# Attention kernel: two PSUM tiles of one bank in place of one tile of two banks, and a normalising step in two halves, one step later

## The chip, the cores and the metric

One core of one Trainium2 chip runs the whole program. The metric is the time of one execution on the device in microseconds (us). The engines have their own in-order queues and run side by side: TensorE (PE) multiplies and transposes, VectorE (DVE) and ScalarE (ACT) do elementwise work, GpSimd (POOL) does small elementwise work, SyncE (SP) issues DMA transfers. PE writes its results to PSUM, which is divided into banks of 512 float32 values per partition; DVE and ACT read them from there.

## The reference

Three blocks follow each other; only the first is touched by the change. It is attention over 4 batches and 8 heads, with 576 positions and heads of 64 values, and a threshold in place of a full softmax:

```python
scores = scale * np.matmul(q, k.transpose(0, 1, 3, 2))
thresh = np.max(scores, axis=-1, keepdims=True) - tau
scores = np.where(scores >= thresh, scores, -1000000000.0)
scores = scores - np.max(scores, axis=-1, keepdims=True)
attn = np.exp(scores)
attn = attn / (np.sum(attn, axis=-1, keepdims=True) + 1e-09)
return np.matmul(attn, v)
```

Its output, as a table of 2304 tokens by 512 values, goes through a gated block (two products, a sigmoid, a product) and a second block with another activation, both with weights in float32.

## The kernel before

Attention works on **pairs of heads** (p = 0 to 15) and, in each pair, on five **units** u: units 0 to 3 are 128 query rows of both heads, unit 4 is the 64 rows left over of each head, stacked. One turn of the loop at L384 is a **step**; a step starts unit u of pair p and carries older units on. The order of the instructions on each engine is the order in which the code issues them; a scheduling layer adds only the waits between engines. In one step, in this order:

- PE multiplies queries with keys for the new unit (`scores`, L245, for unit 4 L241) into two PSUM tiles, transposes the masked exponents of the unit from two steps ago (`turns`: L288 for the first 512 keys, into the wide tile; L289 for the last 64 keys of both heads, into `left`), and multiplies transposed exponents with values (`attend`, L312), into `av`. Once a pair, in the step of unit 2, L401 also transposes the row sums into another part of `left`.
- DVE scales the scores and takes their extreme (`maxima`, L254), then, for the unit of the step before, makes the masked exponents and their sum (`masks`, L274).
- ACT copies the transposes out of PSUM (`copies`: L294 and L298, for unit 4 twice L303 and L304; L298 and L304 read `left`), then takes the exponentials of the new unit (`exponents`, L266), then, when a round of products with values is complete, copies it out of `av` (`drain`, L322), and once a pair copies the row sums out of `left` (`sum_rows`, L331).
- POOL makes the thresholds (L257), copies the last keys' exponents together (`lt`, L281), and once a pair multiplies a finished pair of heads by the reciprocals of its sums (`normalise`, L342), which came back by DMA (`spread`, L339).

The products with values of a pair come in two rounds (table at L378): round 0 is complete in the step in which the next pair starts unit 1, round 1 in the step in which it starts unit 4. Both rounds use the same place `av`, so the first product of a round has to wait until the drain of the round before is done. `left` and `av` are the two halves of one tile `aw`, each half one bank. Parts of the later blocks' work (weights split into two words, L138 and L148 to L162) are spread over the attention steps, one piece in the step of unit 0 of each pair.

Step 0, step 1 and so on below mean the step in which a pair starts unit 0, unit 1 and so on.

Of the kernel before, what the change touches and what calls it, by code (L numbers as in the profile page):

```python
# [10 lines left out]
F32 = mybir.dt.float32  # L11
# [3 lines left out]
ALU = mybir.AluOpType  # L15
AX = mybir.AxisListType
PSUM = bass.MemoryType.PSUM
# [12 lines left out]
def kernel(  # L30
# [17 lines left out]
    nc = tc.nc  # L48
# [3 lines left out]
    NP, _, S = q.shape  # L52
# [5 lines left out]
    P = 128  # L58
    HS = S // 2
# [8 lines left out]
    pool = lambda n, b, **kw: tc.tile_pool(name=n, bufs=b, **kw)  # L68
# [14 lines left out]
    rbs = [const.tile([P, S], F32, name=f"rb_{i}") for i in range(2)]  # L83
# [109 lines left out]
    def attention():  # L193
# [2 lines left out]


        ps_o = ctx.enter_context(ExitStack())
        aw = ps_o.enter_context(pool("ps_o", 1, space=PSUM)).tile([P, 2, 512], F32, name="aw")
        left, av = aw[:, 0], aw[:, 1]  # L200
        wa, wb, wt = wides
        st1, st2 = (ctx.enter_context(ExitStack()) for _ in range(2))
        sb1 = lambda n, b: st1.enter_context(pool(n, b))
# [5 lines left out]
        N = NP * U  # L209
# [7 lines left out]
        def load(p):  # L217
            t = qkp.tile([P, 2, S], F32, tag="qk", name="qk")
            nc.sync.dma_start(out=t[:, 0], in_=q[p])
            nc.sync.dma_start(out=t[:, 1], in_=k[p])  # L220
            qk[p] = t

        def load_v(p):

            t = vs[p % 3]
            for e in range(2):
                es = slice(e * R, e * R + R)
                nc.sync.dma_start(out=t[:, e, :nf], in_=v[p][:, e * (nf + 1) : e * (nf + 1) + nf])
                nc.sync.dma_start(out=t[es, e, nf], in_=v[p][es, nf])

        def corner(p):
            for e in range(2):
                es = slice(e * R, e * R + R)
                nc.gpsimd.tensor_copy(corners[p % 2][es, es], qk[p][es, 0, nf * P :])

        def scores(p, u):
            t = qk[p]
            for s in range(2):
                c = slice(s * HS, s * HS + HS)
                if u == nf:  # L240
                    nc.tensor.matmul(wa[:, s, :HS], corners[p % 2], t[:, 1, c], start=True, stop=True)  # L241
                    continue
                for e, w in enumerate((wa, wb)):
                    es = slice(e * D, e * D + D)
                    nc.tensor.matmul(  # L245
                        w[:, s, :HS], t[es, 0, u * P : u * P + P], t[es, 1, c], start=True, stop=True
                    )

        def maxima(p, u):

            t = sp.tile([P, 2, 2, HS], F32, tag="s", name="s")
            mx = mxs[(p * U + u) % 2]
            for e, w in enumerate((wa, wb)[: 1 if u == nf else 2]):
                nc.vector.tensor_scalar(  # L254
                    t[:, e], w[:, :, :HS], nscale, None, op0=ALU.mult, op1=ALU.min, accum_out=mx[:, 0, e : e + 1]
                )
                nc.gpsimd.tensor_scalar(  # L257
                    mx[:, 1, e : e + 1], mx[:, 0, e : e + 1], tau_b, None, op0=ALU.add
                )
            st[p, u] = t, mx  # L260

        def exponents(p, u):
            t, mx = st[p, u]
            ex = pe_.tile([P, 2, 2, HS], F32, tag="ex", name="ex")
            for e in range(1 if u == nf else 2):
                nc.scalar.activation(ex[:, e], t[:, e], AF.Exp, scale=-1.0, bias=mx[:, 0, e : e + 1])  # L266
            st[p, u] = t, mx, ex
# [15 lines left out]
        def turns(p, u):  # L283
            pr = pt.pop((p, u))
            for e in range(1 if u == nf else 2):
                for c in range(nf):
                    cs = slice(c * P, c * P + P)
                    nc.tensor.transpose(wt[:, e, cs], pr[:, e, cs], ident)  # L288
            nc.tensor.transpose(left[:, :P], lts.pop((p, u)).rearrange("p a b -> p (a b)"), ident)  # L289

        def copies(p, u):
            r, o = min(u // 2, 1), u % 2 * P if u < nf else 2 * P
            if u < nf:
                nc.scalar.activation(  # L294
                    rt[r].rearrange("p e c n -> p (e c) n")[:, :, o : o + P],
                    wt.rearrange("p e (c n) -> p (e c) n", n=P), AF.Copy,
                )
                nc.scalar.activation(rl[r][:, o : o + P], left[:, :P], AF.Copy)  # L298
                return
            for e in range(2):  # L300
                es = slice(e * R, e * R + R)
                x = wt[:, 0].rearrange("p (c n) -> p c n", n=P)
                nc.scalar.activation(rt[r][:, e, :, o : o + R], x[:, :, es], AF.Copy)  # L303
                nc.scalar.activation(rl[r][es, o : o + R], left[es, es], AF.Copy)  # L304

        def attend(p, r, cs):


            n = NR[r]
            for c in cs:  # L310
                for e in range(2):
                    nc.tensor.matmul(  # L312
                        av[e * D : e * D + D, :n], vs[p % 3][:, e, c], rt[r][:, e, c] if c < nf else rl[r],
                        start=c == 0, stop=c == nf,
                    )

        def x_of(p):
            b, hp = divmod(p, NHP)
            return xall[:, hp, b * S : (b + 1) * S]

        def drain(p, r):
            nc.scalar.activation(x_of(p)[:, r * NR[0] : r * NR[0] + NR[r]], av[:, : NR[r]], AF.Copy)  # L322

        def denom(p):
            rs = sums[p % 2]
            nc.vector.reciprocal(rs, rs)

        def sum_rows(p):

            n = 2 * nf + 1  # L330
            nc.scalar.activation(rows[p % 2][:n], left[:n, P : 2 * P], AF.Copy)  # L331
            drs[p] = dram.tile([n, P], F32, tag="dr", name="dr")
            nc.sync.dma_start(out=drs[p], in_=rows[p % 2][:n])
# [4 lines left out]
                src = bass.AP(tensor=dr.tensor, offset=dr.offset + o, ap=[[a, 2], [0, D], [1, n]])  # L338
                nc.sync.dma_start(out=rbs[p % 2][:, (o > 0) * nf * P :][:, :n], in_=src)  # L339

        def normalise(p):
            nc.gpsimd.tensor_tensor(x_of(p), x_of(p), rbs[p % 2], op=ALU.mult)  # L342

        def background():

# [35 lines left out]
        for p in range(NP):  # L381
            for i, (r, a, b) in (rounds if p + 1 < NP else final).items():
                parts.setdefault(p * U + i, []).append((p, r, range(a, b)))
        for t in range(N + 7):  # L384
            p, u = divmod(t, U)
            on = t < N
            mk = divmod(t - 1, U) if 1 <= t <= N else None
            at = divmod(t - 2, U) if 2 <= t <= N + 1 else None

            pd, ud = divmod(t - U, U)  # L390
            pd2, ud2 = divmod(t - 2 * U, U)
            if ud2 == 1 and 0 <= pd2 < NP:
                normalise(pd2)
            if on:
                scores(p, u)
            if t == N + 1:
                yield t - N, True
            if at:
                turns(*at)
            if ud == 2 and 0 <= pd < NP:  # L400
                nc.tensor.transpose(left[: 2 * nf + 1, P : 2 * P], sums[pd % 2], ident)  # L401
            for part in parts.get(t, ()):
                attend(*part)
            if on:
                maxima(p, u)
            if at:
                copies(*at)
            if on:
                exponents(p, u)
            if ud == 1 and 0 <= pd < NP:  # L410
                denom(pd)
            if on and u == 0 and p > 0:
                if p < 13:
                    next(bg, None)
                else:
                    yield t - N, "gap"
            if ud == 2 and 0 <= pd < NP:
                sum_rows(pd)
            for part in parts.get(t, ()):
                if part[2][-1] == nf:  # L420
                    drain(*part[:2])
            if mk:
                masks(*mk)
                if mk[1] == nf:
                    nc.gpsimd.tensor_scalar(sums[mk[0] % 2], sums[mk[0] % 2], 1e-9, None, op0=ALU.add)
            if on:
                if u == 1 and p + 1 < NP:
                    corner(p + 1)
                if u == 2 and p + 2 < NP:
                    load(p + 2)  # L430
                if u == 4 and p + 2 < NP:
                    load_v(p + 2)
                if t == 1 or u == 2 and p % 2 == 0 and p < 12:
                    next(bg, None)
            if ud == 3 and 0 <= pd < NP:
                spread(pd)
            if t == N - 1:
                wides[:] = [wb, wa, wt]
            if t == N:
                run(bg)  # L440
                nc.scalar.activation(dummy, half, AF.Sigmoid)
                st1.close()
            if t == N + 2:
                st2.close()
                ps_o.close()
            yield t - N, False
# [267 lines left out]
```

## Time and profile before

| | us |
|---|---|
| median of 3 runs (1171.86 to 1172.95) | 1172.07 |
| time of the profiled execution | 1175.26 |
| span of the profiled execution | 1173.1 |
| PE busy in the span | 1137.0 (97%) |
| DVE busy | 804.2 (69%) |
| ACT busy | 563.5 (48%) |
| POOL busy | 139.9 (12%) |

The median is from runs without the profiler; the profiled execution is another one. Attention takes up the first 310 us or so of the span; a pair of heads takes about 18.4 us there. The rest belongs to the two later blocks. Busy shares over the whole span mix these stages, so what follows reads the attention stage by itself.

### The profile page before, as it was taken

What the parts mean: (1) busy time and instruction counts of PE and PEld (TensorE: products, weight loads), DVE (VectorE), ACT (ScalarE), POOL (GpSimd) and SP (SyncE); (2) the same over time, 40 slices, a digit from 0 to 9 for tenths busy, and PEclk for the clock granted to TensorE, in tenths of its full rate; (3) what the DMA queues carried; (4) which work ended last, traced back from release to release, by engine and by line L of the source; (5) the groups of instructions that cost most, each with busy time, mean ns of one, the idle gap of its engine ahead of it and who ended that gap; (6) DMA issues with size and microseconds to landing.
All of it is one profiled execution on the core that took longest, in us unless ns stands there. A gap on an engine that the chain in (4) does not pass through costs nothing.

```text
span 1173.1 us, 17522 instructions
## 1 busy us (share of the span) xinstructions
PE 1137.0 (97%) x6516; PEld 969.1 (83%) x6516; DVE 804.2 (69%) x1491; ACT 563.5 (48%) x1027; POOL 139.9 (12%) x299
## 2 busy tenths in 40 slices
PE   8999999998899999999999999999999999999998
PEld 5555555555689999999999999998989898989897
DVE  6888888888499998756667654455556555575554
ACT  5777777777534434333344332344345434353433
POOL 3444444445100000000000000000000000000000
PEclk8999999999989999999999999999999999999999
DMA  3232232220556556444344324112110512041201
GB/s 127 81 79 71 70 100 63 61 73 21 176 182 211 179 180 225 157 166 162 135 162 161 138 87 142 39 54 67 60 54 16 177 60 64 27 152 65 62 11 54
DMA packets 59380, 122.31 MB, mean 104 GB/s; under 512 B 8976, under 2 KB 35232, under 8 KB 59296
## 3 DMA queue, kind: packets, MB, share of 16 engines
q1 hardware_dynamic: 59152, 121.20, 31.6%
q8 instruction: 51, 0.84, 0.3%
q14 instruction: 33, 0.27, 0.1%
q10 hardware_dynamic: 144, 0.00, 0.0%
HBM read 98.57 MB, written 22.62 MB: 103 GB/s over the span
## 4 chain that ended last, share of the span: by engine, by line
PE 85%; DVE 9%; ACT 2%; issue 2%; DMA 1%; POOL 0%; DVEq 0%; SPq 0%; POOLq 0%; ACTq 0%
PE w L562 17%; PE w L554 13%; PE pgv L471 8%; PE pgv L473 8%; PE pgv L472 8%; PE pu L473 6%; PE pu L472 6%; PE pu L471 6%; PE aw L312 5%; PE w L245 4%; DVE s L254 3%; PE w L288 3%; DVE p L274 2%; PE w L241 1%; ACT ex L266 1%
## 5 line engine op out<-in xcount | busy, mean ns | idle before, releaser
L471 PE MATMUL pgv<-xflat,ih 128*128 128x384 f32 x560 | 188.6, 337 | 6.1 <-ACT act L513 4.2
L473 PE MATMUL pgv<-xflat,il 128*128 128x384 f32 x560 | 188.3, 336 | 0.0
L472 PE MATMUL pgv<-xflat,ih 128*128 128x384 f32 x560 | 188.3, 336 | 0.0
L528 ACT ACTIVATE hh<-act 128x384 fp32r<-128x384 f32 x168 | 88.5, 527 | 180.8 <-DVE act L517 119.0
L254 DVE TENSOR_SCALAR_CACHE_REDUCE s<-w,nscale 128x576 f32<-128x576 f32 x144 | 112.7, 816 | 40.4 <-PE w L245 28.9
L524 ACT ACTIVATE act<-act,half 128x384 f32<-128x384 f32 x96 | 59.2, 617 | 167.7 <-DVE act L521 167.7
L530 DVE TENSOR_TENSOR hl<-act,hh 128x384 fp32r<-128x384 f32 x168 | 93.5, 557 | 62.0 <-ACT hh L528 62.0
L473 PE MATMUL pu<-xflat,il 128*128 128x384 f32 x384 | 128.9, 336 | 0.0
L472 PE MATMUL pu<-xflat,ih 128*128 128x384 f32 x384 | 128.9, 336 | 0.0
L471 PE MATMUL pu<-xflat,ih 128*128 128x384 f32 x384 | 128.5, 335 | 0.0
L517 DVE TENSOR_TENSOR act<-pgv,act 128x384 f32<-128x384 f32 x70 | 38.9, 555 | 118.8 <-PE pgv L473 115.2
L274 DVE SCALAR_TENSOR_TENSOR p<-s,mx,ex 128x576 f32<-128x576 f32 x144 | 119.0, 859 | 0.5 <-POOL lt L281 0.5
L562 PE MATMUL w<-oh,hh 128*128 128x512 f32 x288 | 113.9, 395 | 0.4 <-DVE xall L585 0.4
L562 PE MATMUL w<-ol,hh 128*128 128x512 f32 x288 | 114.0, 396 | 0.0
L562 PE MATMUL w<-oh,hl 128*128 128x512 f32 x288 | 113.9, 396 | 0.0
L471 PEld LDWEIGHTS pgv<-xflat,ih 128*128 128x128 f32 x560 | 105.9, 189 | 8.5 <-ACT act L513 4.8
L266 ACT ACTIVATE ex<-s,mx 128x576 f32<-128x576 f32 x144 | 104.5, 770 | 6.7 <-DVE s L254 6.3
L472 PEld LDWEIGHTS pgv<-xflat,ih 128*128 128x128 f32 x560 | 106.0, 189 | 1.8 <-DVE xflat L463 0.2
L473 PEld LDWEIGHTS pgv<-xflat,il 128*128 128x128 f32 x560 | 105.8, 189 | 0.0
L525 DVE TENSOR_TENSOR act<-pu,act 128x384 f32<-128x384 f32 x96 | 53.5, 558 | 70.2 <-ACT act L524 70.2
L288 PEld LDWEIGHTS w<-ident,p 128*128 128x128 f32 x576 | 63.5, 142 | 43.2 <-ACT ex L266 31.2
L513 ACT ACTIVATE act<-pgv 128x384 f32<-128x384 f32 x70 | 34.2, 489 | 134.7 <-PE pgv L473 134.5
(82 smaller groups left out, 2189.3 us busy)
## 6 DMA issues: line engine op xcount, KB each, us to landing
w<-saved SPq DMA_DIRECT2D x48, 512.0 KB
w<-saved SPq DMA_DIRECT2D x24, 768.0 KB
raw<-in_moe_w_out_dram SPq DMA_DIRECT2D x28, 512.0 KB
saved<-w SPq DMA_DIRECT2D x12, 768.0 KB
raw<-in_moe_w_in_dram SPq DMA_DIRECT2D x16, 512.0 KB
saved<-w SPq DMA_DIRECT2D x16, 512.0 KB
raw<-in_moe_w_gate_dram SPq DMA_DIRECT2D x12, 512.0 KB
raw<-in_moe_w_val_dram SPq DMA_DIRECT2D x12, 512.0 KB
```

What stands on the lines that cost most here:

```text
L254: nc.vector.tensor_scalar(t[:, e], w[:, :, :HS], nscale, None, op0=ALU.mult, op1=ALU.min, accum_out=mx[:, 0, e : e + 1])
L266: nc.scalar.activation(ex[:, e], t[:, e], AF.Exp, scale=-1.0, bias=mx[:, 0, e : e + 1])
L274: nc.vector.scalar_tensor_tensor(pr[:, e], t[:, e].rearrange("p a b -> p (a b)"), mx[:, 1, e : e + 1], ex[:, e].rearrange("p a b -> p (a b ...
L288: nc.tensor.transpose(wt[:, e, cs], pr[:, e, cs], ident)
L471: nc.tensor.matmul(ps, ih[:, i, kk], xh[:, kk, c], start=(kk == 0), stop=False)
L472: nc.tensor.matmul(ps, ih[:, i, kk], xl[:, kk, c], start=False, stop=False)
L473: nc.tensor.matmul(ps, il[:, i, kk], xh[:, kk, c], start=False, stop=(kk == KD - 1))
L524: nc.scalar.activation(act, act, AF.Square, scale=0.5, bias=half)
L528: nc.scalar.activation(hh[:, c], act, AF.Copy)
L530: nc.vector.tensor_tensor(hl_[:, c], act, f32(hh[:, c]), op=ALU.subtract)
L554: nc.tensor.matmul(at(y, a, b), l[:, ds_], r[:, c], start=new and m == 0, stop=last and m == 2, skip_group_check=True,)
L562: nc.tensor.matmul(y[i % 3][:, i // 3], l[:, ts_], r, start=first and m == 0, stop=last and m == 2,)
```

## The change

The tile `aw` of two banks becomes two tiles `left` and `av` of one bank each, in the same pool. The multiplication by the reciprocals, one instruction over 576 columns in step 1 two pairs later, becomes two instructions over 288 columns, one in step 2 and one in step 3. The loop runs two turns longer so that the last pair gets both halves. From L341 on the line numbers of the kernel after are higher by one.

```diff
-        aw = ps_o.enter_context(pool("ps_o", 1, space=PSUM)).tile([P, 2, 512], F32, name="aw")
-        left, av = aw[:, 0], aw[:, 1]
+        banks = ps_o.enter_context(pool("ps_o", 1, space=PSUM))
+        left, av = (banks.tile([P, 512], F32, name=n) for n in ("left", "av"))
...
-        def normalise(p):
-            nc.gpsimd.tensor_tensor(x_of(p), x_of(p), rbs[p % 2], op=ALU.mult)
+        def normalise(p, s):
+            x, c = x_of(p), slice(s * HS, s * HS + HS)
+            nc.gpsimd.tensor_tensor(x[:, c], x[:, c], rbs[p % 2][:, c], op=ALU.mult)
...
-        for t in range(N + 7):
+        for t in range(N + 9):
...
-            if ud2 == 1 and 0 <= pd2 < NP:
-                normalise(pd2)
+            if ud2 in (2, 3) and 0 <= pd2 < NP:
+                normalise(pd2, ud2 - 2)
```

On POOL, this is the stretch from step 1 to step 3 of one pair before (`xall` is the attention output, `rb` the reciprocals, `mx` the thresholds, `corner` the stacked queries of unit 4):

```order
L342 TENSOR_TENSOR xall<-xall,rb_80 128x576
L257 TENSOR_SCALAR mx_83<-mx_83,tau_b 128x1 x2
L281 COPY lt<-p 128x128
L234 COPY corner_81<-qk 64x64 x2
L257 TENSOR_SCALAR mx_84<-mx_84,tau_b 128x1 x2
L281 COPY lt<-p 128x128
L257 TENSOR_SCALAR mx_83<-mx_83,tau_b 128x1 x2
```

The same stretch of the kernel after:

```order
L257 TENSOR_SCALAR mx_83<-mx_83,tau_b 128x1 x2
L281 COPY lt<-p 128x128
L234 COPY corner_81<-qk 64x64 x2
L343 TENSOR_TENSOR xall<-xall,rb_80 128x288
L257 TENSOR_SCALAR mx_84<-mx_84,tau_b 128x1 x2
L281 COPY lt<-p 128x128
L343 TENSOR_TENSOR xall<-xall,rb_80 128x288
L257 TENSOR_SCALAR mx_83<-mx_83,tau_b 128x1 x2
```

The multiplication no longer stands ahead of the thresholds of step 1; a half of it stands behind the corner copies, and the other behind the `lt` copy of step 2.

On PE, this is the middle of step 2 before, with the semaphores that each instruction waits for in brackets (`w_123` is the wide tile, `p` the masked exponents, `r` their transposes, `v` the values):

```order
L288 MATMUL w_123<-ident,p 128x128 [waits DVE_49]
L288 MATMUL w_123<-ident,p 128x128 x3
L289 MATMUL aw<-ident,lt 128x128 [waits Activation_49,Pool_49]
L401 MATMUL aw<-ident,sum_87 9x128
L312 MATMUL aw<-r_159,v_164 64x320 x4
```

The same place in the kernel after:

```order
L288 MATMUL w_123<-ident,p 128x128 [waits DVE_49]
L288 MATMUL w_123<-ident,p 128x128 x3
L289 MATMUL left<-ident,lt 128x128 [waits Activation_49,Pool_49]
L402 MATMUL left<-ident,sum_87 9x128
L312 MATMUL av<-r_160,v_165 64x320 [waits Activation_49]
L312 MATMUL av<-r_160,v_165 64x320 x3
```

The first product with values now has a wait for ACT of its own, which before stood two instructions ahead of it, on the transpose into the other bank. The order of PE's instructions is the same.

## Rows read from the trace of the kernel before

**Rows 1.** Window: us, busy PE, PEld, DVE, ACT, POOL, PE clock, DMA share, GB/s.
```profile
200.00:250.00 50.00, 46.34 (x328) 28.53 (x326) 43.78 (x108) 36.72 (x69) 23.61 (x47) 1.00 0.27 72
```

**Rows 2.** Waits of PE, 30 to 310 us: total us, times, longest.
```profile
PE w L288 <- DVE p L274: 9.2, 11, 1.0
PE aw L289 <- POOL mx L257: 5.0, 8, 0.6
PE aw L289 <- ACT xall L322: 3.7, 8, 0.6
```

**Rows 3.** Waits of ACT, 30 to 310 us.
```profile
ACT rl L298 <- PE aw L312: 20.6, 31, 1.8
ACT rl L304 <- PE aw L312: 16.9, 14, 1.2
```

**Rows 4.** Timeline, steps 1 and 2 of one pair: start, us, engine, line, count, [idle before].
```profile
211.13 0.27 PE L289 MATMUL aw<-ident,lt 128*128 128x128 f32 x1
211.33 1.08 PE L312 MATMUL aw<-r,v 128*64 128x256 f32 x8
211.33 0.38 ACT L303 ACTIVATE r<-w 128x256 f32<-128x256 f32 x1 [0.87 <-PE w L288]
...
212.92 0.22 ACT L304 ACTIVATE rl<-aw 64x64 f32<-64x64 f32 x1 [1.21 <-PE aw L312]
...
213.68 1.44 ACT L266 ACTIVATE ex<-s,mx 128x576 f32<-128x576 f32 x2
...
213.95 1.24 PE L288 MATMUL w<-ident,p 128*128 128x128 f32 x8
...
214.61 0.29 POOL L281 COPY lt<-p 128x128 f32<-128x128 f32 x1
...
215.15 0.38 ACT L322 ACTIVATE xall<-aw 128x256 f32<-128x256 f32 x1
...
215.67 0.30 PE L289 MATMUL aw<-ident,lt 128*128 128x128 f32 x1 [0.49 <-ACT xall L322]
...
216.01 1.30 PE L312 MATMUL aw<-r,v 128*64 128x320 f32 x8
```

**Rows 5.** Timeline, step 3 of the same pair.
```profile
218.41 1.09 PE L288 MATMUL w<-ident,p 128*128 128x128 f32 x8
218.51 0.82 DVE L254 TENSOR_SCALAR_CACHE_REDUCE s<-w,nscale 128x576 f32<-128x576 f32 x1 [0.86 <-PE w L245]
...
219.34 0.27 PE L289 MATMUL aw<-ident,lt 128*128 128x128 f32 x1
```

**Rows 6.** Timeline, step 2 of the first such pair.
```profile
30.73 1.10 PE L288 MATMUL w<-ident,p 128*128 128x128 f32 x8
32.45 0.30 PE L289 MATMUL aw<-ident,lt 128*128 128x128 f32 x1 [0.62 <-ACT xall L322]
```

**Rows 7.** Timeline, step 2 of the last such pair.
```profile
287.68 1.09 PE L288 MATMUL w<-ident,p 128*128 128x128 f32 x8
...
288.87 0.38 ACT L322 ACTIVATE xall<-aw 128x256 f32<-128x256 f32 x1
...
289.40 0.30 PE L289 MATMUL aw<-ident,lt 128*128 128x128 f32 x1 [0.62 <-POOL mx L257]
```

**Rows 8.** Timeline, DVE and POOL in step 1 of the pair of rows 4.
```profile
211.39 0.81 DVE L254 TENSOR_SCALAR_CACHE_REDUCE s<-w,nscale 128x576 f32<-128x576 f32 x1
211.71 1.41 POOL L342 TENSOR_TENSOR xall<-xall,rb 128x576 f32<-128x576 f32 x1 [0.42 <-DMA rb<-dr]
212.25 1.48 DVE L274 SCALAR_TENSOR_TENSOR p<-s,mx,ex 128x576 f32<-128x576 f32 x1
```

**Rows 9.** All masks of the kernel: shortest, median, longest, in ns.
```profile
L274 DVE SCALAR_TENSOR_TENSOR p<-s,mx,ex x144: 759/815/1625, 11.1 to 298.6; 128x576 f32<-128x576 f32 x144
```

**Rows 10.** Timeline of ACT at the end of attention.
```profile
311.62 0.27 ACT L331 ACTIVATE row<-aw 9x128 f32<-9x128 f32 x1 [3.54 <-PE aw L312]
311.80 0.41 ACT L322 ACTIVATE xall<-aw 128x320 f32<-128x320 f32 x1
```

## The prediction

> **What bounds the kernel now.** I read the attention stage alone, since the diff touches nothing else: first the busy times by window, then PE's waits, then ACT's, then the timeline of one pair. The window shows PE busy for 46.34 of 50 us at a granted clock of 1.00 (its level of 2.4 GHz), DVE for 43.78 [rows 1]. Two engines are nearly full, so what matters is where PE stands still all the same. Its waits fall into two places [rows 2]: L288 in step 1, where DVE's masks come late (9.2 us in 11 times), and L289 in step 2 (5.0 and 3.7 us, 16 times, one per pair). The change touches the second.
>
> Follow the second back in one pair [rows 4]. L289 starts at 215.67, right after the drain L322 ended (215.15 + 0.38 = 215.53). The drain stands on ACT behind the two exponentials L266 (213.68), these behind the copies L303 and L304, and the first L304 stood idle for 1.21 us until L312 was through, at about 212.9. But L304 reads `left`, which L289 had finished at 211.13 + 0.27 = 211.40; L312 writes the other bank. So both ends of this chain are waits that the data doesn't ask for: L304 for products in `av`, and L289 for the drain of `av`. ACT's waits show that it is so everywhere: L298 and L304 wait for L312 45 times [rows 3]. In 8 pairs the wait view names POOL's L257 as what ended L289's wait; the drain does there too, for in the last pair it ends at 288.87 + 0.38 = 289.25 and L289 starts 0.15 us later [rows 7], against 0.14 in rows 4.
>
> **The split of the tile.** It removes both waits. I work the pair of rows 4 through.
>
> ACT: L303 starts at 211.33 and ends at 211.71; L304 can follow at once. From the first L304 to the first L266 it took 213.68 - 212.92 = 0.76 us, so L266 starts at 212.47 in place of 213.68. Its scores are there: the second L254 of that step ends at 211.39 + 0.81 = 212.20 [rows 8]. The drain follows 215.15 - 213.68 = 1.47 later, at 213.94, and ends at 214.32, 1.21 us earlier. The products that it reads end at 212.9, so its new wait for PE is met.
>
> PE: step 2 reaches L288 at 213.95. How long from there to L289 if nothing waits? Step 3 shows it: 219.34 - 218.41 = 0.93 us, against 215.67 - 213.95 = 1.72 in step 2 [rows 4, 5]. So L289 starts at 214.88, and the pair gains 0.79 us. The new wait, of L312 for the drain, costs nothing: L312 comes 216.01 - 215.67 = 0.34 after L289, at 215.22, and the drain ended at 214.32. What is queued behind L312 on PE are the next step's scores, which DVE waits for; they move 0.79 forward. What is late next? The copy `lt`, which ended at 214.61 + 0.29 = 214.90 [rows 4]: level with the new start of L289. It follows a mask which the other part of the change lets go up to 0.66 us earlier (below), so it won't hold.
>
> Does the gain stay? From step 3 to step 0 of the next pair PE has no wait in the wait view, so what it gains in step 2 it carries forward. DVE must keep up: it stands idle 0.86 us before the first L254 of step 3, waiting for PE [rows 5]. PE comes 0.79 earlier and the masks ahead of it about 0.56 (0.66, less a short wait for scores), so 0.63 us of idling stays. The other wait, L288 in step 1, stays as it is: it hangs on DVE's work after the scores of step 0, and these move along with PE.
>
> The distance from L288 to L289 in step 2 is 1.72 us in 13 of the 15 pairs that have it (32.45 - 30.73 in the first, 289.40 - 287.68 in the last [rows 6, 7]), and 0.03 and 0.08 less in the other two. The sum is 15 x 0.79 - 0.11 = 11.7 us. The sixteenth entry of rows 2 is in the last steps; there the wait is 0.15 us and I count nothing.
>
> At the end of attention L331 waits for L312 although its row sums are long there, and the drain L322 stands behind it [rows 10]. L331 will be done before; the drain starts at 311.62 and no longer at 311.80, and with it ACT's first work for the next block, queued behind: 0.2 us.
>
> What it adds: a wait on the first L312 of each round. Those of step 0 already have a wait for a DMA and so get a wait instruction. L289 waits for two engines in every step, and step 3's 0.93 us holds that wait, already met, so I take 0. The ends are 0 and what a wait takes to let PE go when it is met late, 0.14 us in rows 4: 15 x 0.14 = 2.1 us.
>
> **The normalising.** Before, L342 runs on POOL from 211.71 to 213.12, and the mask L274 beside it takes 1.48 us in place of the median of 0.815: 0.66 more, while the L254 that also runs beside it keeps its 0.81 [rows 8, 9]. So a POOL multiplication holds up a mask, and not a maximum. Without it DVE is 0.66 earlier with that pair of masks, and then waits for the scores of step 2. In step 3 the waiting L254 starts 0.10 us after PE's L288 [rows 5], so here it starts at 213.95 + 0.10 = 214.05. That is what lets `lt` go earlier (above). The delay was hidden by the drain; with the drain gone it would have kept about 0.1 us in this pair. The move thus protects the 0.79 more than it adds.
>
> Where do the halves fall? Half of 1.41 is 0.71 us. The first stands behind the corner copies; POOL gets there about 0.9 us after the last mask of step 1, which is at about 214.7, while DVE runs its two L254 of step 2 (214.05 to 215.5). The second stands behind the `lt` copy of step 2, at about 217.5, when DVE idles or runs the L254 of step 3. So neither is beside a mask, and both cost 0. The ends are 0 and 0.71 us for each half that does hold up a mask. The thresholds behind them are wanted a step later, and the reciprocals, for which L342 still stood idle 0.42 us, have one step more.
>
> The trace agrees with the lock that the Trainium skill describes (SBUF — State Buffer, "Who interferes with whom"): a DVE instruction with two inputs from SBUF and a GpSimd instruction that reads SBUF exclude each other, and the one that starts first holds the port to its end. By that rule cutting one instruction in two makes two occasions for a mask to be held; if both take one, that is the third rival below.
>
> **Sum.** 11.7 + 0.2 = 11.9 us less. The profiled execution took 1175.26 us, 3.2 more than the median of the plain runs; from it 1163.4, and against the median of 1172.07 it is **1160.2 us**.
>
> **Rivals.**
> 1. The wait only moves. If the exponentials of step 1 start late for another reason, the drain ends when it did, and L312 waits in place of L289. Then L289 and L401 run under the wait, 0.34 us a pair: 15 x 0.34 = 5.1, 1167.0 us. For it: the drain still stands behind two exponentials. Against: I find 214.32 against a need at 215.22, so 0.9 us would have to go wrong.
> 2. DVE becomes the bound. It is 88% busy, and of its idle time in step 3 I leave 0.63 us. If half of the gain is lost that way, it is 15 x 0.4 = 6 us, 1166 us. Against: all of DVE's waits in steps 3, 4 and 0 are for PE.
> 3. The port: each half starts just before a mask and holds it up for 0.71 us. That is 1.41 a pair, less DVE's 0.63 of idling, 0.78, which cancels the 0.79: 1172 us. For it: a half and the masks of step 1 are 0.1 us apart on my timetable. Against: even if the first half does hit, its delay lies within the 0.63.
> 4. Slower: PE is held while ACT reads `left`. Before, no L298 or L304 ran beside L312, so no row shows this pair. If every such read stops PE for its length (four of 0.28 us and two of 0.22 in a pair), that is 1.56 a pair, 15 x (1.56 - 0.79) = 11.6 us more, 1183.7 us; it decides from half of that price on. Against: L303 reads PSUM beside L312 in rows 4 with no gap in PE, and L294 reads it beside L312 in every other step.
> 5. The waits are not what they look like, and the split changes nothing: 1172 us. Against: the new program has the waits at their new places.
>
> **How the numbers follow.** The forecast 0.80, with a range of its own of 1157.5 to 1164.5: below, 0.2 us a pair more if the wait in step 1 shrinks as well; above, the 2.1 us of waits and one half of the normalising that costs its 0.71 in three pairs. Rival 1 0.07, rival 2 0.05, rivals 3 and 5 0.05 together, rival 4 0.03. A measurement here can tell about 0.2% (2.3 us) from no change. Faster is the forecast with rivals 1 and 2: 0.92; same 0.05; slower 0.03. The range is drawn from 1157 to 1167.5, to take in rivals 1 and 2.
>
> **What would show it.** In the profile after: L304 starts behind L303 with no wait for L312; L322 in step 1 ends before PE reaches L312 of step 2; L288 to L289 in step 2 takes 0.93 us; no mask over 0.85 us; a pair takes 17.6 us rather than (289.40 - 32.45) / 14 = 18.35; L288 in step 1 still waits for DVE, 0.7 to 0.95 us. I am wrong if L312 of step 2 waits for L322 (rival 1), if DVE is never idle in step 3 (rival 2), if masks are still stretched (rival 3), or if L312 grows (rival 4).

## The result and the profile after

The changed kernel takes 1160.31 us (median of 4 runs, 1159.82 to 1160.6), the kernel before on the same chip 1172.51 us (1171.86 to 1173.05). The ratio is 0.9896, with a 95% interval of 0.9879 to 0.9913: 12.2 us less. The forecast was 1160.2 us.

The span of the profiled execution went from 1173.1 to 1158.7 us, which is 2.2 us more than the medians give. PE's granted clock was 0.88 in the first 29.3 us of the profiled execution before and is 1.00 in the first 30 us of the one after. That isn't the change: of the kernels below that keep the one tile, the one with the multiplication alone has 1.00 there, and the one with the drain early 0.89. So I compare inside attention, from the first L401 (L402 after) to the one 14 pairs later.

The windows of attention after, in the columns of rows 1, for the same 50 us: PE is busy 1.1 us longer in them, at the same clock.

```profile
200.00:250.00 50.00, 47.46 (x337) 29.50 (x334) 43.88 (x114) 37.60 (x72) 25.27 (x55) 1.00 0.24 66
```

The waits of PE and of ACT after, 30 to 310 us (total us, times, longest), against rows 2 and 3. The waits of L289 are gone; that of L288 for DVE is what it was (9.2 us). On ACT, L298 and L304 wait for PE no more; the idle time is now in front of L294, where ACT simply waits for its next transposes.

```profile
PE w L288 <- DVE p L274: 9.1, 11, 1.0
PE w L288 <- ACT ex L266: 2.8, 3, 1.0
...
ACT r L294 <- PE w L288: 46.8, 56, 1.0
ACT r L303 <- PE w L288: 18.8, 15, 2.9
ACT xall L322 <- PE av L312: 3.9, 2, 2.6
```

The timeline of steps 1 to 3 of one pair after (start, us, engine, line), against rows 4, 5 and 8:

```profile
201.46 0.27 PE L289 MATMUL left<-ident,lt 128*128 128x128 f32 x1
...
201.66 0.38 ACT L303 ACTIVATE r<-w 128x256 f32<-128x256 f32 x1 [1.09 <-PE w L288]
...
201.94 0.21 ACT L304 ACTIVATE rl<-left 64x64 f32<-64x64 f32 x1
...
204.15 0.39 ACT L322 ACTIVATE xall<-av 128x256 f32<-128x256 f32 x1
...
204.28 1.09 PE L288 MATMUL w<-ident,p 128*128 128x128 f32 x8
...
205.06 0.79 POOL L343 TENSOR_TENSOR xall<-xall,rb 128x288 f32<-128x288 f32 x1
...
205.21 0.27 PE L289 MATMUL left<-ident,lt 128*128 128x128 f32 x1
...
205.52 1.30 PE L312 MATMUL av<-r,v 128*64 128x320 f32 x8
...
207.84 0.80 POOL L343 TENSOR_TENSOR xall<-xall,rb 128x288 f32<-128x288 f32 x1
...
208.02 0.82 DVE L254 TENSOR_SCALAR_CACHE_REDUCE s<-w,nscale 128x576 f32<-128x576 f32 x1 [0.57 <-PE w L245]
```

L304 runs right behind L303, 0.48 us after the transpose that it reads began, and 1.3 us earlier against L303 than in rows 4 (0.28 us after it, before 1.59). The drain ends at 204.15 + 0.39 = 204.54, and PE reaches the product that needs it at 205.52. From L288 to L289 it is 205.21 - 204.28 = 0.93 us. Before, it was 1.72.

### The profile page after: what moved, and what is told of

Read it like the earlier page. It is cut to its first block, busy times and chain, and to the rows that moved or that the text cites. A ratio compares the mean times of both kernels' runs of the same rounds, so it can differ in the third digit from the quotient of the medians.

```text
span 1158.7 us, 17531 instructions
## 1 busy us (share of the span) xinstructions
PE 1131.9 (98%) x6516; PEld 968.6 (84%) x6516; DVE 796.9 (69%) x1491; ACT 559.5 (48%) x1027; POOL 137.6 (12%) x315
## 4 chain that ended last, share of the span: by engine, by line
PE 90%; DVE 6%; issue 2%; ACT 2%; DMA 1%; POOL 0%; DVEq 0%; ACTq 0%; POOLq 0%
PE w L563 17%; PE w L555 13%; PE pgv L472 8%; PE pgv L473 8%; PE pgv L474 8%; PE av L312 6%; PE pu L474 6%; PE pu L473 6%; PE pu L472 6%; PE w L288 5%; PE w L245 5%; DVE s L254 2%; PE w L241 2%; DVE p L274 1%; DVE high L158 1%
## 5 line engine op out<-in xcount | busy, mean ns | idle before, releaser
L254 DVE TENSOR_SCALAR_CACHE_REDUCE s<-w,nscale 128x576 f32<-128x576 f32 x144 | 112.7, 816 | 33.7 <-PE w L245 23.9
L274 DVE SCALAR_TENSOR_TENSOR p<-s,mx,ex 128x576 f32<-128x576 f32 x144 | 112.0, 810 | 0.5 <-POOL lt L281 0.5
L288 PEld LDWEIGHTS w<-ident,p 128*128 128x128 f32 x576 | 62.8, 141 | 41.6 <-ACT ex L266 36.6
```

Of the source, the lines that this page charges most:

```text
L254: nc.vector.tensor_scalar(t[:, e], w[:, :, :HS], nscale, None, op0=ALU.mult, op1=ALU.min, accum_out=mx[:, 0, e : e + 1])
L274: nc.vector.scalar_tensor_tensor(pr[:, e], t[:, e].rearrange("p a b -> p (a b)"), mx[:, 1, e : e + 1], ex[:, e].rearrange("p a b -> p (a b ...
```

## The experiments

All times are medians of 4 to 11 runs, and each ratio is to the kernel before on the same chip (medians of 1172.55 to 1172.81 us). The time of a pair of heads, below, is the distance between L401 (or the same line under its new number) in the first pair and 14 pairs later, divided by 14.

**The split alone.** The tile is split as in the change; the multiplication stays as it was.

```diff
-        aw = ps_o.enter_context(pool("ps_o", 1, space=PSUM)).tile([P, 2, 512], F32, name="aw")
-        left, av = aw[:, 0], aw[:, 1]
+        banks = ps_o.enter_context(pool("ps_o", 1, space=PSUM))
+        left, av = (banks.tile([P, 512], F32, name=n) for n in ("left", "av"))
```

> Only the tile is split; the multiplication by the reciprocals stays whole in step 1. Theory (the two waits between left and av are the loss): step 2's stretch from L288 to L289 falls from 1.72 to about 0.95 us, with some 0.1 us a pair lost where a stretched mask holds the lt copy; 1161 us, up to 1164 if the reciprocals, which come by DMA, now land late for a faster step 1. Rival (moving the multiplication off the masks carries a good part): 1166 us or more.

Measured: 1159.57 us (1159.26 to 1160.7), ratio 0.989 (0.9876 to 0.9903). A pair takes 17.54 us, as in the changed kernel. The whole gain is the split's. Not even the 0.1 us a pair that I had put down to the other part is missing. The timeline of step 1 and 2 of a pair in this kernel shows why:

```profile
200.87 1.42 POOL L342 TENSOR_TENSOR xall<-xall,rb 128x576 f32<-128x576 f32 x1
...
201.73 1.17 DVE L274 SCALAR_TENSOR_TENSOR p<-s,mx,ex 128x576 f32<-128x576 f32 x1
...
203.78 0.29 POOL L281 COPY lt<-p 128x128 f32<-128x128 f32 x1
...
204.36 0.27 PE L289 MATMUL left<-ident,lt 128*128 128x128 f32 x1
...
207.17 0.82 DVE L254 TENSOR_SCALAR_CACHE_REDUCE s<-w,nscale 128x576 f32<-128x576 f32 x1 [0.35 <-PE w L245]
```

The mask is still stretched (1.17 us), but less than in rows 8, since L342 no longer starts late for its reciprocals. The pair of rows 4 was one of four in which it did; in 8 of 14 pairs the mask already took only 1.14 to 1.15 us before, and in the split alone it takes 1.14 to 1.26. `lt` is done at 204.07, 0.29 us before PE wants it. What the stretch costs comes off DVE's idle time in step 3: 0.35 us are left of the 0.57 of the changed kernel.

**The multiplication alone.** The halves in steps 2 and 3, the tile as before (the new `normalise` and the two turns more of the loop as in the change, not shown again):

```diff
...
-            if ud2 == 1 and 0 <= pd2 < NP:
-                normalise(pd2)
+            if ud2 in (2, 3) and 0 <= pd2 < NP:
+                normalise(pd2, ud2 - 2)
```

> Only the multiplication is cut and moved to steps 2 and 3; the tile stays one of two banks. Theory: masks are no longer stretched, DVE gets 0.3 to 0.66 us a pair, but L289 still waits for the drain, so no change, 1172 us (within 2.5). Rival (the masks held by POOL were the loss): up to 15 x 0.66 = 10 us less, 1162 us.

Measured: 1172.86 us (1171.98 to 1175.38) against 1172.63, ratio 1.0001 (0.9992 to 1.001). No change, and a pair takes 18.35 us as before. DVE's time saved turns into longer waits for PE's scores: its L254 waited 23.9 us for L245 before, and 32.5 here. PE's waits, 30 to 310 us, show the drain in its old place:

```profile
PE aw L289 <- ACT xall L322: 7.0, 12, 0.6
...
PE aw L289 <- POOL xall L343: 2.5, 4, 0.6
```

With the multiplication gone from step 1, the wait view names the drain in 12 cases and not in 8, and something else of POOL's in 4. The name was the last event before PE went on and not always the cause.

**The drain early, with one tile.** The tile and the multiplication as before; ACT gets the drain ahead of the step's exponentials.

```diff
+            for part in parts.get(t, ()):
+                if part[2][-1] == nf:
+                    drain(*part[:2])
             if on:
                 exponents(p, u)
...
-            for part in parts.get(t, ()):
-                if part[2][-1] == nf:
-                    drain(*part[:2])
```

> The tile stays one of two banks and the multiplication stays whole; the drain is issued on ACT ahead of the step's exponentials. Theory (L289 waits for the drain because both touch one tile, and L312 has to wait for it anyway): the drain of step 1 ends about 1.5 us earlier though L304 still waits for L312, PE gains 0.66 to 0.79 us a pair, 1161 to 1163 us. Rival (what counts is that L304 and L298 wait for L312 and hold the exponentials): those waits stay, 1170 us or more.

Measured: 1161.38 us (1160.0 to 1164.17), ratio 0.9906 (0.9893 to 0.992); a pair takes 17.58 us. ACT's waits, 30 to 310 us:

```profile
ACT rl L304 <- PE aw L312: 18.1, 15, 1.2
...
ACT rl L298 <- PE aw L312: 10.6, 31, 1.4
```

L304, which stands ahead of the exponentials of step 1, waits for L312 as long as it ever did (L298 in the other steps waits half as long as in rows 3), the masks are stretched as they ever were, and the time comes down nearly as far. So the rival falls: what cost the time was not that the copies waited, but that the drain ended after PE wanted it. The split moves the drain forward by freeing the copies ahead of it; issuing it earlier does the same.

What is missing to the split alone, 0.04 us a pair in the traces, lies in three pairs, which take 0.08, 0.08 and 0.43 us longer than there. In these three L342 had stood idle for 0.35 to 0.70 us and held the mask for so long that PE had to wait for it in step 2. The third of them:

```profile
204.37 1.41 POOL L342 TENSOR_TENSOR xall<-xall,rb 128x576 f32<-128x576 f32 x1 [0.70 <-DMA rb<-dr]
...
204.63 1.76 DVE L274 SCALAR_TENSOR_TENSOR p<-s,mx,ex 128x576 f32<-128x576 f32 x1
...
206.55 1.31 PE L288 MATMUL w<-ident,p 128*128 128x128 f32 x8
...
207.69 0.27 PE L289 MATMUL aw<-ident,lt 128*128 128x128 f32 x1
```

The mask ends at 206.39, 0.16 us before L288, and L289 follows 1.14 us after L288 and not 0.93. Masks that end 0.44 us before L288 or earlier, as all do in the split alone, cost nothing there.

**The drain late, with two tiles.** The changed kernel; the drain of round 0 is issued behind the copies of step 2 (which therefore stand ahead of `attend` there).

```diff
-        parts = {}
+        parts, late = {}, []
...
+            if late:
+                copies(*at)
+                drain(*late.pop())
+                at = None
             for part in parts.get(t, ()):
                 attend(*part)
...
                 if part[2][-1] == nf:
-                    drain(*part[:2])
+                    if part[1] == 0 and on:
+                        late.append(part[:2])
+                    else:
+                        drain(*part[:2])
```

> The changed kernel, with the drain of round 0 issued on ACT behind the copies of step 2, so that it ends about 206.9 on the time scale of the changed kernel's trace, where L312 of step 2 starts at 205.52. Theory (PE's wait for the drain is not gone but met early, now at L312): L312 waits until about 207.0, 1.5 us a pair, 15 x 1.5 = 22 us more than the changed kernel, 1183 us. Rival (with two tiles PE no longer depends on the drain): 1160 us.

Measured: 1181.65 us (1181.29 to 1181.8), ratio 1.0076 (1.0062 to 1.009), 21 us more than the changed kernel and more than the kernel before. PE's longest waits, 30 to 310 us:

```profile
PE av L312 <- ACT xall L322: 20.1, 15, 1.3
```

The timeline of one step 2:

```profile
218.39 0.27 PE L289 MATMUL left<-ident,lt 128*128 128x128 f32 x1
...
219.67 0.39 ACT L322 ACTIVATE xall<-av 128x256 f32<-128x256 f32 x1
...
220.11 1.30 PE L312 MATMUL av<-r,v 128*64 128x320 f32 x8 [1.34 <-ACT xall L322]
```

L289 has long been through and L312 starts 0.05 us after the drain's end (219.67 + 0.39 = 220.06). The wait is where the prediction had it: at L312, no longer at L289, and free only as long as the drain comes in time.

**The multiplication whole, in step 2.** The split, and the multiplication in one piece a step later (the loop runs one turn longer):

```diff
...
-            if ud2 == 1 and 0 <= pd2 < NP:
+            if ud2 == 2 and 0 <= pd2 < NP:
                 normalise(pd2)
```

> The tile is split; the multiplication stays whole and moves to step 2. Theory: it runs beside the two L254 and then beside the first mask of step 2, which it stretches by up to 0.66 us; DVE's idle time in step 3 (0.63 us by the prediction) takes nearly all of that, 1160 to 1163 us. Rival (a held mask goes straight to PE): 15 x 0.66 = 10 us more than the changed kernel, 1170 us.

Measured: 1160.19 us (1159.21 to 1160.56), ratio 0.9894 (0.9879 to 0.9909). The timeline of steps 2 and 3:

```profile
204.11 1.42 POOL L342 TENSOR_TENSOR xall<-xall,rb 128x576 f32<-128x576 f32 x1
...
204.91 1.23 DVE L274 SCALAR_TENSOR_TENSOR p<-s,mx,ex 128x576 f32<-128x576 f32 x1
...
207.07 0.82 DVE L254 TENSOR_SCALAR_CACHE_REDUCE s<-w,nscale 128x576 f32<-128x576 f32 x1 [0.18 <-PE w L245]
```

A mask is stretched by 0.42 us, and DVE's idle time in step 3 falls to 0.18 us; PE notices nothing. Whole in step 2, or in halves in steps 2 and 3: it makes no difference while DVE has that time.

**The other wait: background work behind the mask.** The changed kernel still loses 9.1 + 2.8 us at L288 in step 1. There the mask of unit 4 stands on DVE behind a piece of the later blocks' work. This kernel issues that piece behind the mask:

```diff
-            if on and u == 0 and p > 0:
-                if p < 13:
-                    next(bg, None)
-                else:
-                    yield t - N, "gap"
...
             if mk:
                 masks(*mk)
...
+            if on and u == 0 and p > 0:
+                if p < 13:
+                    next(bg, None)
+                else:
+                    yield t - N, "gap"
```

> The changed kernel, with the background piece of step 0 issued behind that step's mask and no longer ahead of it. Theory (PE's remaining wait, L288 in step 1, is the mask standing behind the background piece on DVE; DVE has about 0.6 us a pair to spare elsewhere): that wait, 9.1 + 2.8 us, goes, 1148 to 1150 us. Rival (DVE is nearly full, the piece only pushes the next unit's maxima and masks back, and PE waits in step 2 instead): 1156 us or more.

Measured: 1152.43 us (1150.73 to 1153.54), ratio 0.9826 (0.9812 to 0.9839). The waits at L288 are gone, but only 7.9 us of the 11.9 came out, between what theory and rival had. A pair takes 16.95 us. PE in steps 1 and 2 of one pair:

```profile
209.92 0.66 PE L288 MATMUL w<-ident,p 128*128 128x128 f32 x4
...
211.53 0.60 PE L312 MATMUL av<-rl,v 128*64 128x256 f32 x4
212.06 1.61 PE L245 MATMUL w<-qk 64*128 64x288 f32 x8
```

The scores of step 2 take 1.61 us here where they take 1.24 in the changed kernel: the piece, 1.9 us in this pair (208.93 to 210.83), pushes the maxima of step 1 back, and PE has to wait in the middle of the scores for the tile that they read. It is so in 12 pairs, with 1.35 us in five of them and 1.55 to 1.62 in seven: 3.1 of the 4.0 us that are missing. Where the rest is lost was not followed up. The wait view has this wait not in PE's own rows but in those of its weight loads (PEld), where the changed kernel has no such row:

```profile
PEld w L245 <- DVE s L254: 8.7, 19, 0.5
```

The same with the split alone, the multiplication whole in step 1:

> The same with the tile split but the multiplication whole in step 1, as before. Theory (the move of the multiplication costs nothing as long as DVE has time to spare, and is worth its 0.3 to 0.66 us of held masks once it has none): with the background piece late, DVE has no time to spare in step 1, so this is slower than e5_background_late by 0.2 to 0.4 us a pair, 3 to 6 us: 1152 to 1155 us. Rival (the move is worth nothing in any case): the same as e5_background_late within 1 us.

Measured: 1152.09 us (1151.9 to 1153.33), ratio 0.9828 (0.9815 to 0.9842). I was wrong: the move is not worth 3 to 6 us here, and the medians don't tell the two kernels apart. The traces do: a pair takes 17.01 us and not 16.95, and the difference lies in two of the 14 pairs, 0.28 and 0.50 us. In these two the mask ends 0.15 to 0.16 us before L288 of step 2, as in the late pair of the kernel with the drain early; in the others no mask is held or, twice, one that ends 0.47 us before L288. The second of the two (the view names L322, which ends when the mask does, but L288 waits for DVE's semaphore alone):

```profile
195.37 1.41 POOL L342 TENSOR_TENSOR xall<-xall,rb 128x576 f32<-128x576 f32 x1 [1.41 <-DVE s L254]
...
196.08 1.31 DVE L274 SCALAR_TENSOR_TENSOR p<-s,mx,ex 128x576 f32<-128x576 f32 x1
...
197.55 1.30 PE L288 MATMUL w<-ident,p 128*128 128x128 f32 x8 [0.22 <-ACT xall L322]
...
198.69 0.27 PE L289 MATMUL left<-ident,lt 128*128 128x128 f32 x1
...
201.50 0.82 DVE L254 TENSOR_SCALAR_CACHE_REDUCE s<-w,nscale 128x576 f32<-128x576 f32 x1 [0.19 <-PE w L245]
```

And the background piece late in the kernel before, with one tile and the multiplication whole:

> The kernel before with the background piece late; tile and multiplication as before. Theory (the two waits are separate losses, one in step 1 and one in step 2): 12 us less, 1160 to 1162 us, with L289's wait for the drain as before. Rival (they share one chain, so that taking one away lengthens the other): 1166 us or more.

Measured: 1161.04 us (1159.92 to 1161.66), ratio 0.99 (0.9886 to 0.9913). The time is the theory's, but the two waits are not wholly separate. Each change by itself gives about 12 us, both together 20 (1152.43 us). And L289's wait was not as before: L288 to L289 in step 2 takes 1.14 to 1.72 us here, 1.42 on the mean, and no longer 1.72. So some 4.5 us (15 x 0.30) of this kernel's gain are at the drain's wait, which is shorter with the piece late. Its row in the wait view, against 3.7 us in rows 2:

```profile
PE aw L289 <- ACT xall L322: 1.9, 6, 0.5
```

**Background work spread.** One instruction of it at a time, behind the masks of steps 2, 3 and 4 and of every second step 0, where DVE stood idle. The old places go: step 0, and step 2 of every second pair, which had a piece too. The generator yields after each instruction in place of each third (not shown):

```diff
...
+            if on and u == 0 and p >= 13:
+                yield t - N, "gap"
+            if on and p < 13 and (u >= 2 or u == 0 and p % 2 == 0 and p > 0):
+                next(bg, None)
```

> The changed kernel, with the background work of attention issued one instruction at a time behind the masks of steps 2, 3 and 4 (and, every second pair, step 0), where DVE stood idle 0.24 to 0.57 us a step; the three late pieces for the next block stay in step 0, behind its mask. Theory (with the piece of 1.5 us in one place DVE held the maxima of step 1 and with them PE's scores of step 2, 0.1 to 0.4 us a pair): a pair falls from 16.95 to about 16.75 us, 12 x 0.2 = 2.4 us less than with the piece in one place, 1149 to 1150.5 us. Rival (DVE's idle time is too short for an instruction of 0.4 to 0.7 us, so PE waits for maxima in steps 3, 4 and 0): 1152 us or more.

Measured: 1149.63 us (1146.22 to 1150.39), ratio 0.979 (0.9774 to 0.9805), the fastest of all: 10.7 us less than the changed kernel. A pair takes 16.76 us, and the chain of waits of 150 to 190 us consists of PE alone (start, us, engine, line):

```profile
157.24 1.17 PE w L245 x8
158.41 0.59 PE w L288 x4
159.00 0.11 PE left L289
159.11 1.45 PE av L312 x12
160.56 1.17 PE w L245 x8
161.73 1.02 PE w L288 x8
162.75 0.11 PE left L289
162.86 0.11 PE left L401
```

This stretch of attention is now bounded by PE's own work.

## Why the prediction was right

**The place and the mechanism.** The two waits that the data didn't ask for are gone, L289 stands at 0.93 us after L288 in step 2, and the drain ends 0.98 us before L312 wants it, against 0.90 by the sum. That a late drain would make L312 wait is shown by the kernel with the drain late; that the drain's end is what counts, by the one with the drain early.

**The size.** The sum had 0.79 us a pair. From the first pair to the fifteenth it is 18.35 - 17.54 = 0.81: the 0.79, and the rest because L312 now follows L289 after 205.52 - 205.21 = 0.31 us and no longer 0.34. Fifteen such pairs are 12.2 us, which is the measured difference by itself. For the end of attention I had 0.2 us; there L183 now starts 1.09 us after the last group of L312 (297.88 - 296.79), before 1.25 (312.12 - 310.87), so it is 0.16. For the sixteenth entry, in the last steps, I counted nothing, because its wait was 0.15 us; but from L288 to L289 it took 1.25 us there (297.72 to 298.97) and takes 0.93 (283.97 to 284.90), so it gave 0.32. The new waits cost nothing, as taken. By the traces the gain is thus 12.7 us, the sum had 11.9, and the runs say 12.2, with an interval of 10.2 to 14.2. The mechanism was right; that forecast and median agree within 0.1 us is luck.

The last group of L312 and L183 behind it, in the kernel before:

```profile
310.87 0.71 PE L312 MATMUL aw<-rl,v 128*64 128x320 f32 x4
...
312.12 0.62 ACT L183 ACTIVATE ih<-w 128x512 fp32r<-128x512 f32 x1
```

The same, with what lies between, in the kernel after:

```profile
296.79 0.71 PE L312 MATMUL av<-rl,v 128*64 128x320 f32 x4
...
297.55 0.44 ACT L322 ACTIVATE xall<-av 128x320 f32<-128x320 f32 x1 [2.59 <-PE av L312]
...
297.88 0.62 ACT L183 ACTIVATE ih<-w 128x512 fp32r<-128x512 f32 x1
```

L331 is off this path, as the prediction said; the drain now waits for L312 itself.

**DVE.** The idle time in step 3 was to be 0.63 us and is 0.57. Half of the multiplication was to take 0.71 us and takes 0.79 to 0.80. The first half lies at 205.06 to 205.85 beside the two L254, the second at 207.84 beside idle time and an L254, both as placed. No mask is stretched any more; the longest is 0.85 us (rows 9 had 1.625):

```profile
L274 DVE SCALAR_TENSOR_TENSOR p<-s,mx,ex x144: 756/814/848, 11.5 to 284.8; 128x576 f32<-128x576 f32 x144
```

**The one statement that failed** is that moving the multiplication "protects" the gain, with about 0.1 us in such a pair. It protects nothing here: the split alone is as fast. The 0.1 us rested on the mask being held for 0.66 us, as in the pair of rows 4. But there L342 had waited for its reciprocals; with the split they come in time, and the mask is held for 0.33 to 0.45 us, too little to reach PE. The loss itself is real where L342 starts late and a mask ends late by it: 0.08 to 0.50 us in three pairs of the kernel with the drain early and in two with the background piece late. Over the whole kernel that is 0.6 to 0.8 us, less than the medians can tell.

**The rivals.** The first (the wait only moves) can be had by issuing the drain late; it then costs 21 us against the changed kernel, more than the whole gain. The second (DVE) took nothing of the gain in the changed kernel; it took some, by about 0.2 us a pair, once the background piece let PE go further. The third (the port) is there as an effect, in masks of up to 1.26, 1.33 and 1.31 us in the three kernels with the split and the whole multiplication, none of which is slower by its median than its counterpart with halves. The fourth (PE held while ACT reads `left`): L304 at 201.94 runs beside L312 (201.66), which took 1.08 us, as in rows 4, and L298, at 206.33 for 0.27 us, beside the L312 of step 2 (205.52), which took 1.30, as before.

## What to carry to other kernels

A wait belongs to a tile and not to the bytes that are read: two buffers with separate lives deserve separate tiles even where their banks never meet. Follow such a wait to the one instruction that the busy engine wants last, here a copy out of PSUM, and ask when that one could end; freeing what stands ahead of it and issuing it earlier are then the same gain. A stall of an engine that has idle time before anything waits for its result is worth nothing by itself, however plain it stands in the trace; where a long piece of movable work goes is worth more, and it goes best in pieces as short as the gaps.

## What the runs showed of the hardware

A mask that was held by a POOL multiplication ended 0.61 to 0.62 us after it in every kernel, wherever it had started: 213.73 against 213.12 in rows 8; 202.90 against 202.29 with the split alone; 206.14 against 205.53 with the whole multiplication in step 2; 197.39 against 196.78 with the background piece late and the multiplication whole. Alone it takes 0.81 us. So a mask that is held has done about 0.2 us of its work, no more, whether it is held for 0.36 us or for 0.66; and a POOL multiplication costs DVE the time from the mask's start to its own end, less 0.2 us. A mask that starts in the last 0.2 us is not held: with the background piece late and the halves, one that starts at 46.70 takes 0.81 us, though a half runs until 46.87.

The Trainium skill has a DVE instruction with two inputs in SBUF and a GpSimd instruction that reads SBUF exclude each other (SBUF — State Buffer, "Who interferes with whom"); the runs agree, with this 0.2 us beside it.

Two halves of the multiplication take 0.79 + 0.80 = 1.59 us, and one whole takes 1.41 to 1.42: by that an estimated 0.18 us of an instruction of this kind does not depend on its columns.
